# Windowed attention into an RWKV feed-forward block on one core: the squared keys of the beginning rounded on ScalarE, and the beginning's order written anew

## The chip, the cores and the metric

The kernel runs on one core of a Trainium2 chip. The metric is the device time of one execution in microseconds (us); lower is better. The engines are named as the profile names them: PE is TensorE, which multiplies matrices (PEld is its loading of weights); DVE is VectorE, ACT is ScalarE, POOL is GpSimd, and SP is the engine whose queue issues the transfers. All run side by side, each works through its own queue in order, and they wait for each other by semaphores.

## The reference

Eight batches, eight heads of width 64, 512 local tokens and 32 global ones. Local tokens attend to the global ones and to a window of 32 tokens on each side; global tokens attend to all. What comes out, transposed to tokens by 512 channels, goes through an RWKV channel mix whose value product has the squared keys as input. Cut to what matters:

```python
s_g = scale * q_g @ k_all.T;            out_g = softmax(s_g) @ v_all
s_l = concat(scale * q_l @ k_g.T, where(|i - j| <= 32, scale * q_l @ k_l.T, -1e9))
out_l = softmax(s_l) @ concat(v_g, v_l)
x = concat(out_g, out_l) as (8, 544, 512)       # x_prev: x one token earlier
xk = mu_k * x + (1 - mu_k) * x_prev;    xr = mu_r * x + (1 - mu_r) * x_prev
k = maximum(xk @ w_k, 0)                        # 512 -> 1024
out = sigmoid(xr @ w_r) * ((k * k) @ w_v)       # 512 -> 512, 1024 -> 512
```

## The kernel before

Operands of the feed-forward products are split in two: a high part, rounded to the format fp32r that PE reads, and a low part, the remainder. Each product is then three matmuls: high by high, high by low, low by high. So for a squared key `k2` there are `kkh` (`k2` rounded to fp32r) and `kkl` (`k2 - kkh`); for a mixed input `xkh`, `xkl`, `xrh`, `xrl`; for the weights `wk_h`, `wk_l` and so on. The weights come as 64-bit numbers in 20 chunks of 512 columns and are turned into such pairs on the chip.

The work has a beginning and a steady part. In the beginning, batch 0 is read, attended and mixed, its first keys and gates are computed, batch 1's attention is begun and the 20 chunks of weights are made ready, all interleaved. The steady part takes batches 1 to 7 in loops. The order of the beginning is a string of steps, run one after the other; each appends its instructions to the queues of its engines. So a step's place decides what stands ahead of it on every queue that it uses. A step is a name and its indices. The names that matter here:

- `S`, `G`: scores (PE), per unit of two heads and per half of its blocks, and global scores; `R`, `g`: their scaling and row minimum into `Pt` and `Pg` (DVE); `E`, `X`: exponentials (ACT); `I`, `i`: inverse sums (DVE); `N`, `n`: normalizing (POOL); `T`, `H`: transposes (PE); `C`, `h`: copies of these into `PT` (ACT); `W`: products with the values (PE); `O`: their copies into `xT` (ACT). Without a 1 they belong to batch 0; `S1`, `R1`, `E1`, `T1` and the like to batch 1.
- `c`: load of a weight chunk (SP); `a` and `e`: its two steps on ACT (`L240`, and `L254`, the cast to the high part); `b` and `d`: its two on DVE (`L244`, `L249`); `f`: its low part (POOL, `L258`). Chunks 0 to 7 are `w_k`, 8 to 11 `w_r`, 12 to 19 `w_v`.
- `kd`, `kx`, `kc`, `kl` (token half, first of two groups of channels): the token mix for the keys. `kd` is the difference (DVE, `L665`), `kx` the mix (DVE, `L672`), `kc` the cast to the high part (DVE, `L678`), `kl` the low part (POOL, `L682`). `rd`, `rx`, `rc`, `rl` are the same for the gates.
- `Ka`, `Kb` (half, f): the two halves of a key product (PE, twelve matmuls each); `kr`: relu (ACT, `L618`); `qm`: the square (POOL, `L623`); `z`: the two parts `kkh` and `kkl` (DVE, `L629`, `L630`).
- `Qa`, `Qb`, `y`: gate products (PE) and their tanh (ACT); `Va`, `Vb`, `vo`: value products and the write of a result. `L1`, `M1`: loads of batch 1's queries and keys, and values.

What a step waits for beside its data is a buffer. PSUM has eight banks; in the beginning the products "m" have two, "s" four, and "t" two (`T`, `H`, `W`, part of `G` and, for the second token half, `kd` and `rd` use "t"). The tiles `xfull`, `relu` and `k2` share three buffers, and the weight chunks from the fifth on share four.

Of the kernel before, what the change touches and what calls it, by code (L numbers as in the profile page):

```python
# [69 lines left out]
def local_global_attention_then_rwkv_ffn(  # L70
# [498 lines left out]
    class Tokens:  # L569


        def __init__(self, cur, prev, shape, store):
# [4 lines left out]
        def two(self, pool, name, dtype=F32, tag="tmp"):
# [40 lines left out]
            nc.scalar.activation(self.rk[f0], self.kp.pop(f0), AF.Relu)  # L618

        def key_square(self, f0):  # L620
            rk = self.rk.pop(f0)
            self.k2[f0] = self.two(tmpp, "k2")
            nc.gpsimd.tensor_mul(self.k2[f0], rk, rk)  # L623

        def key_parts(self, f0):
            kh = self.two(mlp, "kkh", F32R, f"kkh{f0}")
# [2 lines left out]
            nc.vector.tensor_copy(kh, k2)  # L629
            nc.vector.tensor_sub(kl, k2, kh.bitcast(F32))  # L630
# [490 lines left out]
    for step in """
        q.0 v.0 q.1 v.1 q.2 v.2 q.3 v.3 mu S.0,0,0 masks c.3 c.0 R.0,0,0 c.1 c.2 E.0,0,0 c.4 S.0,1,0 c.5 c.6 c.8
        R.0,1,0 S.0,0,1 E.0,1,0 G.0 R.0,0,1 E.0,0,1 S.0,1,1 g.0 L1.0 I.0,0 X.0 R.0,1,1 S.1,0,0 N.0,0,1 i.0
        S.1,1,0 E.0,1,1 n.0 N.0,0,0 H.0,0 H.0,1 h.0,0 I.0,1 N.0,1,0 h.0,1 T.0,0,0 T.0,0,1 C.0,0,0 N.0,1,1
        S.1,0,1 C.0,0,1 R.1,0,0 T.0,1,0 S.1,1,1 C.0,1,0 R.1,0,1 T.0,1,1 E.1,0,0 R.1,1,0 G.1 E.1,0,1 R.1,1,1 g.1
        a.3 b.3 X.1 I.1,0 d.3 N.1,0,1 a.0 i.1 b.0 e.3 N.1,0,0 C.0,1,1 d.0 a.1 b.1 W.0,0 f.3 e.0 d.1 E.1,1,0 f.0
        b.2 e.1 b.4 n.1 O.0,0 f.1 b.5 a.2 T.1,0,0 H.1,0 kd.0,0 a.4 C.1,0,0 d.2 h.1,0 T.1,0,1 kx.0,0 e.2 H.1,1
# [222 lines left out]
```

## Time and profile before

| | |
|---|---|
| device time, 3 runs | 645.59, 645.38, 642.23 us, median 645.38 |
| the profiled execution | 643.38 us, of which the span of its instructions 641.6 us |
| PE busy | 617.7 us, 96% of the span |
| DVE, ACT, POOL busy | 80%, 52%, 54% |
| granted clock of TensorE | 0.987 of full speed on the mean; below full in three stretches |
| transfers | 127.13 MB, 198 GB/s on the mean |

From about 92 us on, PE is busy without a break until near the end. Nearly all its idle time and the two long stretches at half clock lie in the beginning, which the change rearranges. The forty slices of the page show this: PE's row reads `5698899999999999999999999999999999999997`, sixteen us a slice. In a timeline, "idle before <- releaser" is what ended the wait.

### The profile page before, as it was taken

What the parts mean: (1) busy time and instruction counts of PE and PEld (TensorE: products, weight loads), DVE (VectorE), ACT (ScalarE), POOL (GpSimd) and SP (SyncE); (2) the same over time, 40 slices, a digit from 0 to 9 for tenths busy, and PEclk for the clock granted to TensorE, in tenths of its full rate; (3) what the DMA queues carried; (4) which work ended last, traced back from release to release, by engine and by line L of the source; (5) the groups of instructions that cost most, each with busy time, mean ns of one, the idle gap of its engine ahead of it and who ended that gap; (6) DMA issues with size and microseconds to landing.
All of it is one profiled execution on the core that took longest, in us unless ns stands there. A gap on an engine that the chain in (4) does not pass through costs nothing.

```text
span 641.6 us, 20381 instructions
## 1 busy us (share of the span) xinstructions
PE 617.7 (96%) x8304; PEld 591.6 (92%) x8304; DVE 515.4 (80%) x1312; ACT 333.9 (52%) x1054; POOL 348.5 (54%) x319
## 2 busy tenths in 40 slices
PE   5698899999999999999999999999999999999997
PEld 3577789999999999999999999999999999999997
DVE  3787999657897699987799697987799677787981
ACT  5996677446273667363746537372746433314211
POOL 6575767436856253765357534755367425652840
PEclk9787999999999999999999999999999999999999
DMA  8944545428356924737373675647372662462775
GB/s 363 368 172 194 179 145 178 155 68 321 122 199 213 340 120 166 231 122 264 143 277 133 238 270 197 214 167 269 121 287 80 214 214 68 148 206 107 234 232 191
DMA packets 43564, 127.13 MB, mean 198 GB/s; under 512 B 4048, under 2 KB 20944, under 8 KB 43472
## 3 DMA queue, kind: packets, MB, share of 16 engines
q1 hardware_dynamic: 43472, 125.85, 55.8%
q8 instruction: 65, 1.06, 0.7%
q14 instruction: 27, 0.22, 0.1%
HBM read 108.53 MB, written 17.30 MB: 196 GB/s over the span
## 4 chain that ended last, share of the span: by engine, by line
PE 88%; DVE 6%; ACT 3%; POOL 2%; issue 1%; POOLq 0%; DVEq 0%; ACTq 0%
PE ps_m L142 68%; PE ps_s L142 12%; PE ps_t L145 5%; PE ps_t L142 1%; DVE Pt L378 1%; ACT Pt L385 1%; DVE kkl L630 1%; DVE ps_t L665 1%; POOL masks L171 1%; DVE kkh L629 1%; DVE xfull L672 1%; POOL Pt L396 0%; ACT wk_h L254 0%; DVE Pg L448 0%; DVE ps_s L665 0%
## 5 line engine op out<-in xcount | busy, mean ns | idle before, releaser
L142 PE MATMUL ps_m<-xkh,wk_h 128*128 128x256 f32 x544 | 155.2, 285 | 0.0
L142 PE MATMUL ps_m<-xkl,wk_h 128*128 128x256 f32 x544 | 151.0, 278 | 0.0
L142 PE MATMUL ps_m<-xkh,wk_l 128*128 128x256 f32 x544 | 150.9, 277 | 0.0
L142 PE MATMUL ps_m<-bh,a 128*128 128x256 f32 x736 | 136.4, 282 | 0.1
L396 POOL TENSOR_TENSOR Pt<-Pt,ssum 128x512 f32<-128x512 f32 x64 | 70.5, 1106 | 94.1 <-DVE ssum L339 60.2
L142 PEld LDWEIGHTS ps_m<-bh,a 128*128 128x128 f32 x736 | 114.7, 189 | 0.3 <-DVE xrh L607 0.3
L385 ACT ACTIVATE Pt<-Pt,m 128x128 f32<-128x128 f32 x256 | 99.4, 392 | 20.2 <-DVE m L378 19.9
L142 PEld LDWEIGHTS ps_m<-xkh,wk_h 128*128 128x128 f32 x544 | 102.5, 188 | 4.0 <-issue 1.4
L142 PEld LDWEIGHTS ps_m<-xkh,wk_l 128*128 128x128 f32 x544 | 102.7, 189 | 0.0
L142 PEld LDWEIGHTS ps_m<-xkl,wk_h 128*128 128x128 f32 x544 | 102.7, 189 | 0.0
L142 PE MATMUL ps_m<-bl,a 128*128 128x256 f32 x368 | 102.6, 279 | 0.0
L142 PE MATMUL ps_m<-xrh,wr_h 128*128 128x256 f32 x272 | 77.0, 283 | 1.0 <-ACT relu L618 1.0
L142 PE MATMUL ps_m<-xrl,wr_h 128*128 128x256 f32 x272 | 75.5, 277 | 0.0
L142 PE MATMUL ps_m<-xrh,wr_l 128*128 128x256 f32 x272 | 75.4, 277 | 0.0
L608 POOL TENSOR_TENSOR xkl<-xfull,xkh 128x512 fp32r<-128x512 f32 x30 | 39.9, 1331 | 60.8 <-DVE xkh L607 33.3
L419 ACT COPY PT<-ps_t 128x512 f32<-128x512 f32 x56 | 32.7, 583 | 76.6 <-PE ps_t L145 76.4
L713 ACT ACTIVATE relu<-ps_m 128x512 f32<-128x512 f32 x52 | 30.7, 591 | 79.8 <-PE ps_m L142 77.6
L142 PEld LDWEIGHTS ps_m<-bl,a 128*128 128x128 f32 x368 | 69.2, 188 | 0.0
L378 DVE CUSTOM_DVE_ANT_0 Pt<-ps_s,masks 128x128 f32<-128x128 f32 x256 | 55.8, 285 | 11.2 <-PE ps_s L142 8.1
L608 POOL TENSOR_TENSOR xrl<-diff,xrh 128x512 fp32r<-128x512 f32 x30 | 41.0, 1368 | 37.9 <-DVE xrh L607 27.6
L798 POOL TENSOR_TENSOR bl<-B,bh 128x512 fp32r<-128x512 f32 x36 | 51.9, 1458 | 16.1 <-DVE bh L797 16.1
L142 PE MATMUL ps_s<-raw_qk 64*32 64x128 f32 (+1 forms) x2112 | 51.7, 287 | 7.6 <-DMA raw_qk<-qk 6.4
(127 smaller groups left out, 1508.2 us busy)
## 6 DMA issues: line engine op xcount, KB each, us to landing
a<-scratch SPq DMA_DIRECT2D x92, 512.0 KB, 4.7
raw_v<-v SPq DMA_DIRECT2D x32, 896.0 KB, 7.3
raw_qk<-qk SPq DMA_DIRECT2D x32, 624.0 KB, 5.4
out_l<-gate SPq DMA_DIRECT2D x32, 256.0 KB, 3.9
w<-w_k SPq DMA_DIRECT2D x8, 512.0 KB, 9.7
w<-w_v SPq DMA_DIRECT2D x8, 512.0 KB, 3.2
w<-w_r SPq DMA_DIRECT2D x4, 512.0 KB, 5.9
scratch<-wv_h SPq DMA_DIRECT2D x8, 256.0 KB, 3.9
```

The source lines that it names most:

```text
L142: return in_line(nc.tensor.matmul(*a, **kw))
L145: return in_line(nc.tensor.transpose(*a, **kw))
L171: nc.gpsimd.affine_select(out=m, in_=m, pattern=[[i - c, CK]], base=0, channel_multiplier=c - i, compare_op=ALU.is_ge, fill=NEG,)
L378: nc.vector.tensor_tensor_reduce(out=self.Pt[:, i], in0=self.place(t, n, h), in1=masks[self.slots[t][1]][:, n], op0=ALU.add, op1=ALU.min, ...
L385: nc.scalar.activation(self.Pt[:, i], self.Pt[:, i], AF.Exp, bias=self.low[:, i:i + 1], scale=-1.0, accum_out=self.sum[:, i:i + 1],)
L396: nc.gpsimd.tensor_mul(self.Pt[:, some], self.Pt[:, some], inv.unsqueeze(2).to_broadcast([P, 4, W]))
L419: nc.scalar.copy(pitched(j, h, 0, 4), tp.rearrange("p (g q) -> p g q", g=4))
L608: nc.gpsimd.tensor_sub(lo[:, both], xf, hi[:, both].bitcast(F32))
L629: nc.vector.tensor_copy(kh, k2)
L630: nc.vector.tensor_sub(kl, k2, kh.bitcast(F32))
L713: nc.scalar.activation(rk, kp, AF.Relu)
L798: (nc.vector if b[0] == "B" else nc.gpsimd).tensor_sub(l, val, h.bitcast(F32))
```

## The change

The rounding of the eight squares `k2` of batch 0 to `kkh` leaves DVE. ACT squares the relu a second time (`key_high`, step `zh`) and writes the result straight in fp32r, so that the write rounds it. `k2` is still made by POOL, and DVE's step `z` keeps only the subtraction `k2 - kkh`. The relu tile therefore stays in use until both POOL and ACT have read it. Besides, the string that orders the beginning is another one throughout; it has the same steps and eight more, the `zh`. The steady part is untouched.

```diff
         def key_square(self, f0):
-            rk = self.rk.pop(f0)
+            rk = self.rk[f0]
             self.k2[f0] = self.two(tmpp, "k2")
             nc.gpsimd.tensor_mul(self.k2[f0], rk, rk)
+        def key_high(self, f0):
+            self.kh[f0] = self.two(mlp, "kkh", F32R, f"kkh{f0}")
+            nc.scalar.activation(self.kh[f0], self.rk[f0], AF.Square)
+
         def key_parts(self, f0):
-            kh = self.two(mlp, "kkh", F32R, f"kkh{f0}")
+            kh = self.kh.pop(f0)
             kl = self.two(mlp if f0 + 2 < NF else mlp1, "kkl", F32R, f"kkl{f0}")
             k2 = self.k2.pop(f0)
-            nc.vector.tensor_copy(kh, k2)
             nc.vector.tensor_sub(kl, k2, kh.bitcast(F32))
...
+        "zh": lambda t, f: first[t].key_high(f),
...
-        d.4 C.1,0,1 f.2 h.1,1 kc.0,0 e.4 W.1,0 a.5 f.4 b.6 a.6 d.5 E.1,1,1 d.6 kl.0,0 c.7 S1.0,0 b.8 O.1,0
-        rd.0,0 Ka.0,0 I.1,1 e.5 rx.0,0 N.1,1,1 e.6 W.0,1 R1.0,0 a.8 f.5 a.7 Ka.0,2 N.1,1,0 rc.0,0 c.9 E1.0,0,0
-        M1.0 f.6 S1.0,1 d.8 O.0,1 I1.0,0,0 kd.0,2 early_w e.8 rl.0,0 T.1,1,0 c.10 G1.0 E1.0,0,1 kx.0,2 kc.0,2
-        L1.1 f.8 a.9 I1.0,0,1 g1.0 C.1,1,0 T.1,1,1 X1.0 kl.0,2 c.11 R1.0,1 C.1,1,1 N1.0,0,1 W.1,1 i1.0 E1.0,1,0
...
+        f.2 c.9 O.1,0 I.1,1 b.7 a.7 Ka.0,2 kd.0,2 e.6 N.1,1,1 a.8 W.0,1 d.7 kx.0,2 e.7 N.1,1,0 a.9 rx.0,0 f.6
+        O.0,1 M1.0 kc.0,2 T.1,1,0 f.7 c.10 T.1,1,1 C.1,1,0 rc.0,0 C.1,1,1 kl.0,2 W.1,1 d.8 early_w e.8 rd.0,2
+        rl.0,0 Kb.0,0 O.1,1 rx.0,2 G1.0 rc.0,2 f.8 kr.0,0 Kb.0,2 zh.0,0 g1.0 qm.0,0 c.11 Ka.0,4 c.12 rl.0,2
+        z.0,0 a.10 S1.0,0 kr.0,2 Kb.0,4 b.9 X1.0 qm.0,2 b.10 zh.0,2 Ka.0,6 d.9 a.11 z.0,2 kr.0,4 e.9 d.10 qm.0,4
+        Kb.0,6 zh.0,4 R1.0,0 e.10 f.9 a.12 kr.0,6 z.0,4 f.10 S1.0,1 c.13 E1.0,0,0 b.11 Qa.0,0 kd.1,0 L1.1
+        E1.0,0,1 qm.0,6 c.14 Qa.0,2 d.11 zh.0,6 kx.1,0 e.11 z.0,6 a.13 f.11 R1.0,1 Qb.0,0 c.15 I1.0,0,1 E1.0,1,0
...
```

Three places show how this moves instructions. The first is ACT ahead of the product `W.1,1`, batch 0's last value product. Before, `L454` (the exponential of batch 1's global scores, `X1.0`) stands between the two copies `L423` (`C.1,1,0` and `C.1,1,1`) that `W.1,1` needs:

```order
L254 CAST wr_h<-w_321 128x512
L385 ACTIVATE Pt,ssum<-Pt,m 128x128 x4
L240 ACTIVATE w_867<-w_867 128x512
L423 COPY PT<-ps_t 128x2x2x128
L454 ACTIVATE Pg,ssumg<-Pg,mg 128x544
L423 COPY PT<-ps_t 128x2x2x128
```

In the change the two copies stand together, right behind the six copies of `O.0,1`, with `e.7` (`w_683`) and `a.9` (`w_758`) ahead of these:

```order
L254 CAST wk_h<-w_683 128x512
L240 ACTIVATE w_758<-w_758 128x512
L539 COPY xT<-ps_t 128x2x64
L542 COPY xT<-ps_t 128x2x32
L549 COPY xT<-ps_t 128x64
L539 COPY xT<-ps_t 128x2x64
L542 COPY xT<-ps_t 128x2x32
L549 COPY xT<-ps_t 128x64
L423 COPY PT<-ps_t 128x2x2x128 x2
L254 CAST wr_h<-w_319 128x512
```

So the exponential left the gap between the copies, and a chunk's step came ahead of the copies before them.

The second is DVE at the same time, at the mix of the first token half's upper channels (`kd.0,2`, `L665`; in the change these lines have numbers three higher). Before, it stands behind the reads of batch 1's first scores (sixteen rows `L378`, not shown) and these:

```order
L678 CAST xrh<-xfull 128x512
L249 SCALAR_TENSOR_TENSOR w_321<-w_321,ps_s 128x512
L338 TENSOR_SCALAR ssum<-ssum 128x4
L339 RECIPROCAL ssum<-ssum 128x4
L665 TENSOR_TENSOR ps_s<-xT 128x256 x2
L672 SCALAR_TENSOR_TENSOR xfull<-ps_s,mu_k_sb,xT 128x256 x2
L678 CAST xkh<-xfull 128x512
```

In the change it follows the inverse sums of batch 0's last scores (`I.1,1`) and `b.7`; `d.7` (`w_683`), which ACT's `e.7` needs, comes behind it:

```order
L338 TENSOR_SCALAR ssum<-ssum 128x8
L339 RECIPROCAL ssum<-ssum 128x8
L244 TENSOR_SCALAR ps_s<-w_683 128x512
L668 TENSOR_TENSOR ps_s<-xT 128x256 x2
L249 SCALAR_TENSOR_TENSOR w_683<-w_683,ps_s 128x512
L675 SCALAR_TENSOR_TENSOR xfull<-ps_s,mu_k_sb,xT 128x256 x2
L675 SCALAR_TENSOR_TENSOR xfull<-ps_s,mu_r_sb,xT 128x256 x2
L681 CAST xkh<-xfull 128x512
```

The eight score reads and one pair of inverse sums went from ahead of it to behind it.

The third is ACT some 15 us later, at the relus of the first keys. Before, the cast `e.11` of the last gate weights (`w_974`) comes right behind the second relu (`L618`):

```order
L254 CAST wr_h<-w_867 128x512
L618 ACTIVATE relu<-ps_m 128x512
L254 CAST wr_h<-w_974 128x512
L240 ACTIVATE w_1144<-w_1144 128x512
L618 ACTIVATE relu<-ps_m 128x512
L482 COPY PT<-ps_t 96x4x2x32
L488 COPY PT<-ps_t 64x4x32
L385 ACTIVATE Pt,ssum<-Pt,m 128x128 x4
```

In the change the same cast (`w_957` there) comes behind the fourth relu, eight exponentials and the fourth new square (`L627`):

```order
L618 ACTIVATE relu<-ps_m 128x512
L254 CAST wr_h<-w_758 128x512
L627 ACTIVATE kkh<-relu 128x512
L254 CAST wr_h<-w_852 128x512
L240 ACTIVATE w_972<-w_972 128x512
L618 ACTIVATE relu<-ps_m 128x512
L385 ACTIVATE Pt,ssum<-Pt,m 128x128 x8
L627 ACTIVATE kkh<-relu 128x512
L254 CAST wr_h<-w_957 128x512
```

So the gate weights' last cast moved behind two more relus, three squares and eight exponentials.

More of the change, by code (lines that the diff above doesn't have):

```diff
@@ L573, in __init__ @@
             self.cur, self.prev, self.shape, self.store = cur, prev, shape, store
-            self.kp, self.rk, self.k2, self.rp, self.vp, self.x, self.d = ({} for _ in range(7))
+            self.kp, self.rk, self.k2, self.rp, self.vp, self.x, self.d, self.kh = ({} for _ in range(8))
             self.kk_h, self.kk_l = [], []
@@ L1121, in local_global_attention_then_rwkv_ffn @@
     for step in """
[L1122 to L1123 removed]
+        q.0 v.0 q.1 q.2 v.1 v.2 q.3 v.3 mu S.0,0,0 masks c.3 c.0 R.0,0,0 c.1 c.4 E.0,0,0 c.5 S.0,1,0 c.6 c.8 c.2
+        R.0,1,0 S.0,0,1 E.0,1,0 G.0 R.0,0,1 E.0,0,1 S.1,0,0 g.0 S.0,1,1 I.0,0 L1.0 X.0 R.0,1,1 N.0,0,1 i.0
         S.1,1,0 E.0,1,1 n.0 N.0,0,0 H.0,0 H.0,1 h.0,0 I.0,1 N.0,1,0 h.0,1 T.0,0,0 T.0,0,1 C.0,0,0 N.0,1,1
@@ L1145, in local_global_attention_then_rwkv_ffn @@
-        f.18 W1.1 N1.2,0,0 e.19 I1.2,1,1 E1.2,1,0 f.19 E1.2,0,1 N1.2,1,1 I1.2,1,0 Vb.0 N1.2,1,0 M1.2 O1.1
-        I1.2,0,1 N1.2,0,1 Vb.2 vo.0 z.1,6 vo.2
+        a.3 b.3 X.1 I.1,0 d.3 N.1,0,1 a.0 b.0 e.3 N.1,0,0 i.1 d.0 C.0,1,1 a.1 b.1 W.0,0 f.3 e.0 d.1 E.1,1,0 b.4
+        n.1 f.0 e.1 b.5 O.0,0 f.1 b.6 a.5 T.1,0,0 H.1,0 kd.0,0 a.4 C.1,0,0 d.4 h.1,0 H.1,1 kx.0,0 e.4 T.1,0,1
+        d.5 a.2 f.4 b.2 h.1,1 C.1,0,1 kc.0,0 e.5 c.7 W.1,0 d.2 kl.0,0 a.6 b.8 e.2 d.6 E.1,1,1 f.5 rd.0,0 Ka.0,0
+        f.2 c.9 O.1,0 I.1,1 b.7 a.7 Ka.0,2 kd.0,2 e.6 N.1,1,1 a.8 W.0,1 d.7 kx.0,2 e.7 N.1,1,0 a.9 rx.0,0 f.6
@@ new lines, in local_global_attention_then_rwkv_ffn @@
+        i1.0 kd.1,2 N1.0,0,1 b.12 S1.1,0 kx.1,2 E1.0,1,1 n1.0 Qb.0,2 I1.0,1,0 kc.1,2 N1.0,1,0 kc.1,0 a.14 G1.1
+        y.0,0 kl.1,2 a.15 I1.0,1,1 T1.0,1,0 I1.0,0,0 g1.1 C1.0,1,0 kl.1,0 y.0,2 H1.0,0 rd.1,0 N1.0,1,1 Ka.1,0
+        X1.1 rx.1,0 h1.0,0 i1.1 N1.0,0,0 Ka.1,2 rc.1,0 rd.1,2 T1.0,1,1 rl.1,0 Kb.1,0 C1.0,1,1 rx.1,2 rc.1,2
+        T1.0,0,0 kr.1,0 H1.0,1 Kb.1,2 rl.1,2 C1.0,0,0 h1.0,1 d.12 zh.1,0 qm.1,0 T1.0,0,1 kr.1,2 b.14 Ka.1,4
+        C1.0,0,1 R1.1,0 zh.1,2 Qa.1,0 early_u e.12 f.12 z.1,0 E1.1,0,1 Kb.1,4 c.16 E1.1,0,0 d.14 Qb.1,0 qm.1,2
@@ new lines, in local_global_attention_then_rwkv_ffn @@
+        b.13 I1.1,0,1 kr.1,4 d.13 S1.1,1 N1.1,0,1 y.1,0 z.1,2 zh.1,4 Qa.1,2 L1.2 e.13 I1.1,0,0 qm.1,4 b.16 a.16
+        Ka.1,6 b.15 e.14 f.13 d.16 Qb.1,2 d.15 e.16 f.14 c.18 R1.1,1 e.15 Kb.1,6 y.1,2 f.16 c.17 W1.0 N1.1,0,0
+        kr.1,6 E1.1,1,0 f.15 z.1,4 zh.1,6 c.19 a.18 b.18 qm.1,6 E1.1,1,1 T1.1,0,0 M1.1 I1.1,1,0 Va.0 d.18
+        N1.1,1,0 e.18 I1.1,1,1 O1.0 N1.1,1,1 n1.1 T1.1,1,0 Va.2 a.19 b.17 f.18 C1.1,1,0 b.19 a.17 d.19 C1.1,0,0
+        d.17 e.19 T1.1,0,1 e.17 f.19 T1.1,1,1 S1.2,0 C1.1,0,1 C1.1,1,1 f.17 H1.1,0 R1.2,0 S1.2,1 h1.1,0 H1.1,1
@@ L1147, in local_global_attention_then_rwkv_ffn @@
+        Vb.0 h1.1,1 R1.2,1 E1.2,0,0 E1.2,0,1 I1.2,0,0 W1.1 N1.2,0,0 vo.0 E1.2,1,0 E1.2,1,1 I1.2,1,0 N1.2,1,0
+        Vb.2 M1.2 O1.1 I1.2,1,1 N1.2,1,1 G1.2 z.1,6 vo.2 g1.2 X1.2 I1.2,0,1 N1.2,0,1 i1.2 n1.2
     """.split():
```

15 lines of the change are left out of this document (removed).

## The prediction

> **What bounds the kernel now.** I read the stretches first, then PE's timeline, then the chain of waits, then the queues of the engines that PE waits for. The stretches are cut at four events of the beginning: the end of `W.0,1`, the first `Kb`, the first `Ka` of the second token half, the first value product. Columns: stretch, length, then busy us (instructions) of PE, PEld, DVE, ACT, POOL, then granted clock, DMA share and GB/s.
>
> ```profile
> 24.00:42.00 18.00, 14.43 (x282) 12.98 (x282) 15.72 (x46) 17.61 (x64) 13.32 (x12) 0.72 0.53 208
> 42.00:54.10 12.10, 8.55 (x149) 6.75 (x148) 11.23 (x38) 7.87 (x34) 8.57 (x8) 0.79 0.97 380
> 54.10:79.20 25.10, 23.07 (x288) 20.06 (x288) 21.57 (x50) 16.81 (x51) 14.91 (x12) 0.96 0.41 141
> 79.20:105.80 26.60, 25.33 (x405) 24.10 (x403) 26.11 (x75) 19.55 (x51) 19.57 (x17) 1.00 0.39 131
> 105.80:121.00 15.20, 15.20 (x215) 14.94 (x210) 9.28 (x36) 11.54 (x50) 9.35 (x9) 1.00 0.69 249
> ```
>
> PE is the bound from 105.8 on. Before that DVE is nearly full (26.11 of 26.60 us in the fourth row) while PE has gaps of 3.55, 2.03 and 1.27 us in rows two to four, and the clock is below full in rows one to three. All that this change can win in the stretches it mainly alters is there: 6.85 us of gaps and what the clock costs. PE's rows name the waits:
>
> ```profile
> 34.36 3.10 PE L142 MATMUL ps_t<-PT,raw_v 128*64 128x96 f32 x80 [0.18 <-ACT PT L423]
> 40.04 2.05 PE L142 MATMUL ps_t<-PT,raw_v 128*64 128x32 f32 x56
> 45.45 0.98 PE L142 MATMUL ps_s<-raw_qk 128*64 128x480 f32 x4
> 48.72 0.30 PE L142 MATMUL ps_t<-PT,raw_v 128*64 128x32 f32 x2 [1.27 <-DVE mg L448]
> 50.93 3.25 PE L142 MATMUL ps_t<-PT,raw_v 128*64 128x32 f32 x54 [1.91 <-ACT PT L423]
> 71.67 0.38 PE L142 MATMUL ps_m<-xrh,wr_h 128*128 128x256 f32 x1 [0.96 <-ACT relu L618]
> 88.67 0.66 PE L145 MATMUL ps_t<-ident,Pt 128*128 128x128 f32 x4 [1.27 <-POOL Pt L396]
> ```
>
> The row at 45.45 is most of `G1.0`. Those at 48.72 and 50.93 are `W.1,1`: 3.18 us of waiting, for a PSUM bank and for a copy. The chain of waits (start, us) shows which engine sets the pace after that, and the price of blocks of matmuls:
>
> ```profile
> 54.18 2.42 PE ps_m L142 x12
> 58.50 1.54 DVE kkh L629
> 65.73 1.49 DVE kkh L629
> 70.25 0.86 DVE kkh L629
> 74.74 0.34 DVE kkh L629
> ...
> 80.69 0.20 DVE Pt L378
> ...
> 101.42 1.38 PE ps_m L142 x12
> 103.13 1.09 PE ps_s L142 x64
> 121.44 0.44 PE ps_t L145 x4
> ```
>
> Four casts to `kkh`, 4.23 us, lie on the chain. Twelve matmuls cost 2.42 us in the stretch with the reduced clock and 1.38 later; `W.1,1` took 3.25 us and the same product `W.0,1` 2.05. So half speed cost 1.04 + 1.20 = 2.24 us here.
>
> **The casts.** Eight go from DVE, eight squares come to ACT; the first two rows group DVE's cast and subtraction, the third is the same square in the steady part, the last two are what POOL did under the first pair:
>
> ```profile
> L629 DVE CAST kkh<-k x8: 410/1098/1529, 58.5 to 119.3; 128x512 fp32r<-128x512 f32 x8
> L630 DVE TENSOR_TENSOR kkl<-k,kkh x8: 691/1568/1776, 60.1 to 121.4; 128x512 fp32r<-128x512 f32 x8
> L715 ACT ACTIVATE B<-relu x52: 630/632/638, 211.8 to 617.3; 128x512 f32<-128x512 f32 x52
> 58.42 1.32 POOL L258 TENSOR_TENSOR wk_l<-w,wk_h 128x512 fp32r<-128x512 f32 x1
> 59.69 1.47 POOL L682 TENSOR_TENSOR xrl<-xfull,xrh 128x512 fp32r<-128x512 f32 x1
> ```
>
> A cast takes 0.41 us alone and up to 1.53 when a POOL instruction runs: the one at 58.50 ended 0.3 us after POOL's of 58.42 did. DVE is freed of 8 x 0.41 to 8 x 1.53, 3.3 to 12.2 us, near 8 by the median of 1.10. ACT gets 8 x 0.63 = 5.1 us, in a queue that was busy 16.81 of 25.10 and 19.55 of 26.60 us, so it has room on the mean. On the path this is worth no more than PE's gaps after 54 us, 2.03 + 1.27: PE had other work under the rest of those 4.23 us.
>
> The Trainium skill speaks against even that (page SBUF — State Buffer, section Who interferes with whom): a DVE cast, and a DVE operation with two SBUF inputs, share a port with GpSimd, and the later one waits for the earlier whole instruction. By that rule the remaining subtraction waits where the cast waited, and only 8 x 0.41 us are surely won. The rows agree that both stretch, 0.41 to 1.53 and 0.69 to 1.78. My sum does not rest on it, since I follow the queues below.
>
> **The order, to `Kb.0,0`.** In the change PE does `Ka.0,0`, `Ka.0,2`, `W.0,1`, `T.1,1,0`, `T.1,1,1`, `W.1,1`, `Kb.0,0`; the two score products `S1.0` and `G1.0` come later. From the end of `W.1,0` (34.36 + 3.10, taken as 37.4) PE has 2 x 1.38 + 2.05 us and is free at 42.2. `T.1,1,0` needs a bank that `O.0,1` empties, and `O.0,1` stands on ACT behind `e.7` and `a.9`. Rows for this walk:
>
> ```profile
> 38.76 0.20 DVE L339 RECIPROCAL ssum<-ssum 128x8 f32<-128x8 f32 x1
> 44.07 2.81 DVE L665 TENSOR_TENSOR ps_s<-xT 128x256 f32<-128x256 f32 x2
> L244 DVE TENSOR_SCALAR ps_s<-w x16: 676/684/712, 28.3 to 109.6; 128x512 int32<-128x512 int32 x16
> L254 ACT CAST wk_h<-w x8: 652/662/710, 24.8 to 57.2; 128x512 fp32r<-128x512 f32 x8
> L240 ACT ACTIVATE w<-w x20: 652/686/784, 22.7 to 109.7; 128x512 f32<-128x512 f32 x20
> 42.64 0.29 ACT L539 COPY xT<-ps_t 128x128 f32<-128x128 f32 x1
> 43.25 0.28 ACT L549 COPY xT<-ps_t 128x64 f32<-128x64 f32 x1
> 50.31 0.56 ACT L423 COPY PT<-ps_t 128x512 f32<-128x512 f32 x1
> 37.71 0.94 DVE L665 TENSOR_TENSOR ps_s<-xT 128x256 f32<-128x256 f32 x2
> ```
>
> `I.1,1` ends at 38.96 as before, then DVE has `b.7` 0.68, `kd.0,2` 0.94 to 2.81 (I take 1.5, nearer the undisturbed pair since fewer POOL instructions lie under it), `d.7` 0.68, to 41.8; ACT has `e.7` 0.66, `a.9` 0.69, the six copies 42.64 to 43.53 = 0.89, to 44.05; then a transpose 0.44 and two copies 1.12: `W.1,1` starts at 45.6, with PE idle 45.6 - 42.2 - 0.88 = 2.5 us against 3.55 before. Gain 1.05, with the ends of `kd.0,2` 1.6 to -0.25. On the clock: it fell after the waits of 1.27 and 1.91 us, so it will probably fall after 2.5, but once, since no second wait follows. I take a loss of 1.5 for the 2.24 of before; ends 0 and 2.24. **Gain to here 1.8, between -0.25 and 3.8.** What covers the moved `S1.0` and `G1.0` is that they fill PE later, one for one.
>
> The Trainium skill (TensorE: Matmul & The Clock Gate, section HAM oscillation) says that the clock falls when PE idles for more than about 3.4 us. By that the gap of 2.5 would cost nothing, and the sum would be 1.5 us better. The trace does not agree: the block of 2.42 us ran at half speed though no wait before it reached 3.4 us (1.27 and 1.91).
>
> **From `Kb.0,0` to `Ka.1,0`.** Before, this took the 25.1 us of the third stretch, for some 20.2 us of matmuls: ten blocks of 1.38, five groups of transposes of 0.44 at most, two score products of 1.09, two global ones of 0.98. Lost are 4.9, of which 1.04 is the clock counted above; 3.85 are left. In the change two waits stand out. `Qb.0,0` needs `f.11` on POOL, behind `e.11`, behind the square `zh.0,6`, behind eight exponentials, behind `kr.0,6`, which waits for `Kb.0,6`:
>
> ```profile
> L385 ACT ACTIVATE Pt<-Pt,m 128x128 f32<-128x128 f32 x256 | 99.4, 392 | 20.2 <-DVE m L378 19.9
> L258 POOL TENSOR_TENSOR wr_l<-w,wr_h x4: 1296/1404/1768, 45.1 to 75.0; 128x512 fp32r<-128x512 f32 x4
> ```
>
> With a relu at the square's 0.63, that is 0.63 + 8 x 0.39 + 0.63 + 0.66 + 1.40 = 6.4 us after `Kb.0,6`, less some 0.3 where ACT's instructions overlap; PE has `S1.0,1` 1.09 and two blocks of 1.38 to do, 3.85, and part of `Qb`: a wait of 2.0. `Ka.1,0` needs `kl.1,0`. After `zh.0,6` (4.2) DVE has a subtraction 0.69, eight reads of 0.21, three inverse sums 1.0, a difference 1.5, `b.12` 0.68, a mix no longer than the pair's undisturbed 0.94 and two casts 0.82; then POOL has two low parts of 1.3: 14 us after `Kb.0,6`. PE arrives 2.8 earlier, part of it already waiting for a transpose. Together 4.8 us, with PE's own small gaps inside them. **A loss of 4.8 - 3.85, about 1.0; the ends are a gain of 3.85, if PE never waits, and a loss of 2.3, if the difference takes 2.81.** The relief of DVE does not show here because `z.0,6` now waits for ACT.
>
> **From `Ka.1,0` to the value products.** The 1.27 us before 88.67 was a transpose that waited for POOL; in the change it comes behind the first value product. I found no new wait: `W1.0` needs the banks of `S1.1,1`, which DVE has read by then. **Gain 1.27; at the other end a new wait as long as the old two of 1.27 and 1.91 less it, a loss of 1.9.**
>
> **Sum.** 1.8 - 1.0 + 1.27 = 2.1 us, from the profiled execution's 643.38: 641.3. Its median of three is 645.38, 2.0 above it, the lowest 642.23. About 0.5%, 3.2 us, is what a measurement of this kernel can tell from no change.
>
> **Rivals.** *No gain:* `kd.0,2` takes 2.81 again, `W.1,1` waits as long and the clock falls for as long; then -0.25 - 1.0 + 1.27, with what DVE saves hidden under PE's other work: about 643.4. For it: the waits moved, their lengths are alike. *All waits go:* DVE, freed of some 8 us, reaches `kc.1,0` early, and PE hardly waits after 42 us: 3.8 + 1.9 (half of the second term's best) + 1.27 = 7.0, 636.4. For it: DVE lay on the chain; against it: ACT's exponentials stand ahead of `zh.0,6`. *The clock stays full* after the gap of 2.5 us, and the rest is as in the sum: 1.5 more, 639.8; for it, the gap stands alone, where before two came together; against it, the fall before. (It is what the page on the clock gate would have.) *Slower:* the transfers of `w_v`. On SP `L1.2` now stands ahead of `c.18`, `c.17`, `c.19`, and its second load waits for `S1.1,1`; `c.19` also for the buffer of `f.15`.
>
> ```profile
> w<-w_v SPq DMA_DIRECT2D x1, 512.0 KB, 3.1
> ```
>
> From the end of `f.15` it takes 3.1 + 0.69 + 0.66 + 0.66 + 2 x 1.3 = 7.7 us till the last low part, and `Vb.0` follows `Va.0` by four blocks of 1.38, two score products and five groups of transposes, some 10 us. So it costs from the point where `f.15` ends more than about 2.3 us after `Va.0` could start, then us for us; with an overrun of 6 and the sum above, 647.
>
> **Chances.** The sum's course 0.38; no gain 0.25; all waits go 0.15; the clock stays full 0.09; slower 0.13. Faster by over 0.5% are the case without waits, the one with the full clock, and 0.16 of the sum's course, which by its own ends can gain over 3.2: 0.40. Slower 0.13, the rest 0.47 the same. The range goes from 636.5, where nearly all waits are gone, to 646.0, no gain and the median's offset; the likeliest case alone 639 to 643.5.
>
> **What would show it.** In the profile after: no `L629` on DVE, eight squares of 0.63 us on ACT; `W.1,1` at 44.5 to 47 with one wait before it; a half-clock stretch shorter than before; PE waiting for POOL's `wr_l` ahead of `Qb.0,0` and for `xkl` ahead of `Ka.1,0`, 4 to 5 us together; no wait of 1 us after that. Wrong would be: no waits in the middle, or one ahead of `Vb.0`.

## The result, and the profile after

The changed kernel takes 648.3 us in the median of 18 runs, the kernel before 644.07 in the median of 18 beside it; the ratio is 1.005, with a 95% interval of 1.0035 to 1.0064. It is slower, by some 3 us, where 2 us of gain were forecast. A second set of 12 runs gave 646.04 us and a ratio of 1.0028 [1.0005 to 1.0052]. Each ratio is to runs of the kernel before beside that set. The profiled execution of the change took 645.9 us (span 644.1), that of before 643.38 (641.6).

The same five stretches of time as in the prediction, after the change; the events that cut them lie elsewhere now (length, then busy us of PE, PEld, DVE, ACT, POOL, granted clock, DMA share, GB/s):

```profile
24.00:42.00 18.00, 13.76 (x160) 12.38 (x161) 16.82 (x30) 16.22 (x59) 13.82 (x12) 0.57 0.61 239
42.00:54.10 12.10, 10.80 (x161) 9.26 (x160) 9.85 (x17) 7.20 (x22) 7.93 (x7) 0.93 0.74 277
54.10:79.20 25.10, 20.15 (x322) 17.58 (x321) 24.42 (x71) 19.18 (x57) 17.36 (x15) 0.97 0.43 144
79.20:105.80 26.60, 26.58 (x358) 25.84 (x357) 21.86 (x67) 20.81 (x65) 18.52 (x16) 0.96 0.46 142
105.80:121.00 15.20, 15.20 (x320) 14.22 (x319) 6.91 (x42) 13.17 (x54) 7.08 (x7) 1.00 0.35 122
```

Over the five DVE is busy 4.1 us less than before: the eight casts, 7.8 us, are gone, but the sixteen subtractions of the mix (`kd`, `rd`) take 3.6 us more. In the fourth row DVE is relieved, 21.86 us instead of 26.11, and PE has next to no gap left. But in the third PE is busy 20.15 us where it was 23.07, with DVE nearly full (24.42 of 25.10), and the clock of the first fell from 0.72 to 0.57. PE's rows that answer to those shown of before:

```profile
34.63 5.17 PE L142 MATMUL ps_t<-PT,raw_v 128*64 128x96 f32 x80 [0.67 <-ACT PT L482]
44.49 1.85 PE L142 MATMUL ps_t<-PT,raw_v 128*64 128x32 f32 x56
47.22 1.06 PE L145 MATMUL ps_t<-ident,Pt 128*128 128x128 f32 x8 [0.88 <-ACT xT L549]
48.52 0.30 PE L142 MATMUL ps_t<-PT,raw_v 128*64 128x32 f32 x2 [0.24 <-ACT PT L423]
49.01 1.85 PE L142 MATMUL ps_t<-PT,raw_v 128*64 128x32 f32 x54 [0.19 <-ACT PT L423]
50.78 0.38 PE L142 MATMUL ps_m<-xkh,wk_h 128*128 128x256 f32 x1
66.78 0.39 PE L142 MATMUL ps_m<-xrh,wr_h 128*128 128x256 f32 x1 [0.61 <-ACT wr_h L254]
68.62 0.39 PE L142 MATMUL ps_m<-xrh,wr_l 128*128 128x256 f32 x1 [1.34 <-POOL wr_l L258]
74.08 0.65 PE L145 MATMUL ps_t<-ident,Pt 128*128 128x128 f32 x4 [0.66 <-POOL Pt L396]
77.07 0.53 PE L145 MATMUL ps_t<-ident,Pg 128*96 128x128 f32 x3 [2.33 <-DVE mg L448]
```

The row at 34.63 is `W.1,0`: 5.17 us instead of 3.10. At 48.52 and 49.01 stands `W.1,1`, with almost no wait before it now, and at full clock (1.85 us, before 3.25). `Kb.0,0` starts at 50.78, before at 54.11, but 3.3 us of score products that were done by then before come later now. Then four waits that were not there, 4.94 us together.

To add up such things I use one figure throughout, the *loss* of a stretch: PE's idle time plus half of its busy time at half speed, from the 12th us on. PE has the same matmuls to do in both orders, so this is, near enough, the time that the order costs.

| loss, us | 12 us to `Kb.0,0` | to `Ka.1,0` | to the first value product | to 130 us | sum |
|---|---|---|---|---|---|
| before | 16.4 | 2.9 | 1.3 | 0 | 20.6 |
| the change | 16.3 | 4.95 | 1.7 | 0.4 | 23.4 |

The difference of 2.8 us is close to the 2.5 us by which the profiled executions differ, and it has all arisen by the first square: that of the steady part (line `L715`, in the change `L718`) starts at 211.8 us before and 214.4 after, and from there on both run alike, to the last one at 617.3 and 619.8.

```profile
L718 ACT ACTIVATE B<-relu x52: 630/632/637, 214.4 to 619.8; 128x512 f32<-128x512 f32 x52
```

The chain of waits shows who sets PE's pace between 62 and 77 us, after the change (start, us):

```profile
63.40 0.87 DVE ps_t L668
64.30 1.15 DVE ps_t L668
...
70.01 1.15 DVE ps_t L668
...
72.81 1.50 DVE xkh L681 x2
74.31 1.16 DVE ssum L338
75.67 1.02 DVE ssum L338
77.07 0.53 PE ps_t L145 x3
```

No cast to `kkh` is on it any more. In their place are differences of the mix (`L668`) and two additions on 128x4 numbers (`L338`) that take as little as 0.14 us elsewhere and took 1.2 and 1.1 here, with POOL busy beside them. DVE itself waits for nothing that counts between 54.3 and 90.0 us: these are all its waits of 0.15 us or more from 54.3 to 91 us.

```profile
61.00 1.79 DVE L633 TENSOR_TENSOR kkl<-k,kkh 128x512 fp32r<-128x512 f32 x1 [0.19 <-POOL k L623]
90.02 0.83 DVE L338 TENSOR_SCALAR ssum<-ssum 128x4 f32<-128x4 f32 x1 [1.21 <-ACT Pt L385]
```

The granted clock by stretches, after (the window's length, PE's busy time, ..., clock):

```profile
26.60:36.80 10.20, 8.01 (x91) 6.69 (x89) 9.52 (x16) 10.00 (x33) 7.22 (x7) 0.50 0.61 242
36.90:40.20 3.30, 3.30 (x53) 3.24 (x52) 3.23 (x6) 1.77 (x13) 2.53 (x3) 0.50 0.54 187
40.30:43.60 3.30, 3.30 (x18) 3.30 (x17) 2.94 (x6) 2.90 (x10) 3.28 (x3) 0.50 0.06 22
74.40:77.70 3.30, 0.97 (x10) 0.73 (x8) 3.09 (x7) 2.14 (x3) 3.30 (x4) 1.00 0.58 192
77.80:81.10 3.30, 3.30 (x18) 3.30 (x17) 3.20 (x10) 1.36 (x4) 0.90 (x2) 0.50 0.00 0
```

Half speed lasts from 26.6 to 43.6 us (before 25.2 to 35.4), the stretch at 49 to 56 is gone, and a new one of 3.4 us follows the waits ahead of `Ka.1,0`.

### The profile page after: what moved, and what is told of

Read it like the earlier page. It is cut to its first block, busy times and chain, and to the rows that moved or that the text cites. A ratio compares the mean times of both kernels' runs of the same rounds, so it can differ in the third digit from the quotient of the medians.

```text
span 644.1 us, 20392 instructions
## 1 busy us (share of the span) xinstructions
PE 620.3 (96%) x8304; PEld 594.2 (92%) x8304; DVE 513.3 (80%) x1304; ACT 338.3 (53%) x1062; POOL 349.9 (54%) x319
## 3 DMA queue, kind: packets, MB, share of 16 engines
q8 instruction: 65, 1.06, 0.7%
## 4 chain that ended last, share of the span: by engine, by line
PE 91%; DVE 3%; ACT 2%; POOL 2%; issue 1%; POOLq 0%; ACTq 0%; DVEq 0%
PE ps_m L142 70%; PE ps_s L142 13%; PE ps_t L145 6%; PE ps_t L142 2%; DVE Pt L378 1%; POOL masks L171 1%; ACT Pt L385 1%; DVE ps_t L668 1%; DVE ssum L338 0%; ACT wk_h L254 0%; ACT PT L423 0%; POOL Pt L396 0%; DVE xkh L681 0%; DVE xfull L675 0%; DVE kkl L633 0%
## 5 line engine op out<-in xcount | busy, mean ns | idle before, releaser
L142 PEld LDWEIGHTS ps_m<-xkh,wk_h 128*128 128x128 f32 x544 | 103.8, 191 | 3.6 <-issue 1.9
L378 DVE CUSTOM_DVE_ANT_0 Pt<-ps_s,masks 128x128 f32<-128x128 f32 x256 | 55.7, 286 | 14.3 <-PE ps_s L142 11.2
L608 POOL TENSOR_TENSOR xrl<-diff,xrh 128x512 fp32r<-128x512 f32 x30 | 41.1, 1370 | 37.3 <-DVE xrh L607 27.3
```

Source lines behind the costliest of these rows:

```text
L142: return in_line(nc.tensor.matmul(*a, **kw))
L378: nc.vector.tensor_tensor_reduce(out=self.Pt[:, i], in0=self.place(t, n, h), in1=masks[self.slots[t][1]][:, n], op0=ALU.add, op1=ALU.min, ...
L608: nc.gpsimd.tensor_sub(lo[:, both], xf, hi[:, both].bitcast(F32))
```

## The experiments

**The square apart from the order.** `e1` has the order of before with the squares on ScalarE; `e2` the new order with the casts on VectorE; `e3` and `e4` cross the two orders at `W.1,0`.

```diff
e1  steps of before; behind each qm.t,f:  + zh.t,f
e2  steps of the change without zh;  z: + nc.vector.tensor_copy(kh, k2)
e3  steps up to W.1,0 as in before, the others in the order of the change
e4  steps up to W.1,0 as in the change, the others in the order of before, with zh
```

> The order of before, with the squares on ScalarE alone (each placed right behind POOL's square of the same tile). Theory A, the loss of 4.2 us (644.1 to 648.3) is PE's clock under the new order, a first half-speed stretch that lasts 17.1 us instead of 10.2 and a new one of 3.4 at Ka.1,0: this kernel has neither, its half-speed stretches stay at 25-35 and 49-56, and it takes 641 to 644.5, since up to 2 us of the casts' 4.2 on the chain come off. Theory B, the squares themselves cost it, by 8 x 0.63 us in ScalarE's queue ahead of what PE waits for: 647 to 648.5. Theory C, the loss is the waits of the new order behind Kb.0,0 alone (1.9 at Qb.0,0, 3.0 ahead of Ka.1,0): as A, 641 to 644.5.

> The order of after, with the casts on VectorE as before and no squares on ScalarE. A: the beginning up to Kb.0,0 has no cast in it, so the clock loss of some 4 us stays, and the four casts of the first half delay VectorE further; 648 to 651. B: without the squares the loss goes, 643.5 to 645.5. C: the waits behind Kb.0,0 grow by 1 to 4 us, since VectorE is the one that reads g1.1 and makes xkh late: 649 to 652, but with a beginning no slower than in before.

> Steps up to W.1,0 in the order of before, all others in the order of after. A: if the order of the first 37 us sets how long the clock stays at half, it ends at about 35 as in before, W.1,0 takes 3.1 us instead of 5.2, the two Ka's 1.4 each, and the kernel takes 644 to 645.5. If it stays down to 42-44 here too, then what comes behind W.1,0 decides it or it is chance from execution to execution, and the time is 647 to 648.5. C: the waits behind Kb.0,0 are untouched, 647.5 to 648.5. B: 648.

> The counterpart: steps up to W.1,0 in the order of after, all others in the order of before, with the squares on ScalarE. A: half speed to about 43, the other waits as in before: 646 to 648. C: no loss without the new order behind Kb.0,0: 642 to 644.5. B: 647 to 648.5.

| | median, us | ratio to before, 95% interval | first steady square, us |
|---|---|---|---|
| e1, square alone | 642.18 | 0.9971 [0.995, 0.9992] | 210.2 |
| e2, order alone | 650.08 | 1.0096 [1.0059, 1.0132] | 217.2 |
| e3, old start, new rest | 649.17 | 1.0078 [1.0049, 1.0107] | 217.1 |
| e4, new start, old rest | 645.73 | 1.001 [0.999, 1.003] | 210.5 |

The square is not the loss: alone it gains 0.3%, some 2 us. Of PE's waits after 54 us the 1.27 is gone, those of 0.96 and 1.01 are 0.42 and 0.51, and one of 0.41 came. The order is the loss, 6 us without the square. In the traces the greater part hangs on what comes behind `W.1,0`: the first steady square is 6.9 us later in e3 than in e1, and 3.9 later in the change than in e4. The start alone is not settled: e4 against e1 is 2 to 3 us in the ratios, but 0.3 in the two traces. Theory B is out, and A, that the order of the first 37 us sets the clock, is not saved: e3 has the old start and the full clock again by 35 us, and is no faster. It is no test of a full clock, since it fell to half speed again from 45.2 to 55.5 and from 72.5 to 75.9 us. Theory C, the waits behind `Kb.0,0`, comes nearest: e2 has the four of the change, grown to 6.3 us, and e4 has none of them; but e3 and e4 both came out above the times that C gave.

**The clock.** `e6` takes away the pause of 0.67 us ahead of `W.1,0`; `e7` fills PE's pauses of 3.5 and 1.4 us with transposes that nothing uses; `e8` does the same in e1's order; `e0` is the change once more.

```diff
e6  - ... d.5 a.2 f.4 b.2 h.1,1 C.1,0,1 ...
    + ... d.5 f.4 b.2 h.1,1 C.1,0,1 a.2 ...
e7  groups(0, shared)                       # W.0,0 only
    + keep_warm(28, both[0])
    groups(0, alone); groups(1, alone); groups(1, shared)
    + keep_warm(18, rest_bank)
```

> The change, with a.2 on ScalarE moved behind the two copies h.1,1 and C.1,0,1, so that W.1,0 comes straight behind the transposes instead of 0.67 us later. Theory A1, the clock's first half-speed stretch is longer in the new beginning since this pause breaks the one dense stretch (30.4 to 34) that could lift it before W.1,0: half speed ends some 7 us earlier in most runs, the granted clock goes from 0.984 to 0.986 to 0.989, and the time falls by 2 to 3.5 us, to 644.5 to 646.5. Rival, the pause has nothing to do with it (where the 3.41-us grid happens to lie, or other work): clock 0.984 and 647.5 to 648.5, 0.6 us better at most.

> The change, with 28 transposes of the identity into an unused quarter of a PSUM bank between the first 24 and the other 56 matmuls of W.0,0, and 18 more behind W.0,0, where TensorE is idle for 3.5 and 1.4 us. They add nothing to the result. Theory A: with no pause over 0.5 us the clock stays full from 13 to 47; W.1,0 takes 2.05 to 3.1 us instead of 5.2, Ka.0,0 and Ka.0,2 take 2.8 instead of 4.7; granted clock 0.992 to 0.995; 3 to 4 us at Kb.0,0 are won if TensorE sets the pace there, 644 to 645.5. Rival, the other engines set the pace to W.1,1 (kd.0,2 and e.8, O.0,1 on their queues): the clock is full, but TensorE waits as much longer ahead of T.1,1,0, and the time is 647 to 648.5. If the filler does not hold the clock, the half-speed stretch stays, and the time is 648 to 649.

> The order of before with the squares on ScalarE (as in the kernel that took 642.2) and the same 28 + 18 transposes of the identity. A: its first half-speed stretch (27.3 to 34.1 in the profile, a loss of 2.2 us by the ledger of pauses and half-speed time) goes, 640 to 641.5; the second one at 51 to 58 stays. Rival, other engines set the pace to W.1,1: 642 to 643.

> The change itself once more, as the measure for the two beside it: 646 to 649. In its profile the half-speed stretch of the beginning may lie elsewhere. If the loss to 50 us (pauses plus half the time at half speed, 13.0 in the first profile) hangs on the clock's chance, it comes out 2 us or more away from 13; if it hangs on the order, it stays within 0.5.

e6: 649.15 us, 1.0064 [1.0042, 1.0087]. e7: 649.6 us, 1.0082 [1.0061, 1.0104], with a granted clock of 0.986 to 0.992 in its runs. e8: 644.27 us, 0.9989 [0.997, 1.0007], no gain on e1 though its clock is 0.994 on the mean of its runs. The profile of e6 says why. Its clock was full from 34.5 to 44.7; `W.0,1` ran at 40.47 instead of 44.49, and then PE stood still:

```profile
40.47 1.85 PE L142 MATMUL ps_t<-PT,raw_v 128*64 128x32 f32 x56
45.54 1.94 PE L145 MATMUL ps_t<-ident,Pt 128*128 128x128 f32 x8 [3.22 <-POOL wk_l L258]
```

`T.1,1,0` needs the bank that the copies `O.0,1` empty, and it starts 0.10 us after the last of them in both profiles (the POOL instruction named in the row is not what it needs). What ACT waited for ahead of these copies differs. In the change it was PE, late by its clock; in e6 it was DVE's `d.7`, which the cast `e.7` ahead of the copies reads. First the change, then e6:

```profile
46.01 0.27 ACT L539 COPY xT<-ps_t 128x128 f32<-128x128 f32 x1 [1.59 <-PE ps_t L142]
```

```profile
43.44 0.66 ACT L254 CAST wk_h<-w 128x512 fp32r<-128x512 f32 x1 [1.90 <-DVE w L249]
```

Of 4 us won 1.7 were left at `T.1,1,0`, and with this pause the clock fell again (1.94 us for eight transposes instead of 1.06), from 44.7 to 54.9, so that `Kb.0,0` came at 51.34 and `Ka.1,0` at 79.52, 0.6 and 2.2 us later than in the change. In e7 and e0 (in this order) the same transposes came about where they came in the change, at 47.22, though `W.1,0` had begun 2 us later; ACT waited for `d.7` there too:

```profile
36.80 4.66 PE L142 MATMUL ps_t<-PT,raw_v 128*64 128x96 f32 x80 [1.15 <-ACT PT L482]
47.42 1.06 PE L145 MATMUL ps_t<-ident,Pt 128*128 128x128 f32 x8 [1.16 <-POOL wk_l L258]
```

```profile
36.63 4.91 PE L142 MATMUL ps_t<-PT,raw_v 128*64 128x96 f32 x80 [0.66 <-ACT PT L482]
47.28 1.06 PE L145 MATMUL ps_t<-ident,Pt 128*128 128x128 f32 x8 [1.04 <-POOL wk_l L258]
```

In e0 the half-speed stretches lay elsewhere (17.2 to 20.6, 27.4 to 41.1, 68.4 to 71.8), and its loss from 12 us to `Kb.0,0` is 16.4, in the first profile 16.3, in e2, e5 and e6 16.3 to 16.4. So theory A falls for this part: up to `Kb.0,0` the order sets the loss, and whether it shows as half speed or as waiting differs from execution to execution. e7 and e8 are no clean tests of the full clock, since filler and a half-speed stretch at 17 to 21 and 16 to 19 us made the work before `W.1,0` late.

**The wait ahead of `Ka.1,0`.**

```diff
- ... zh.0,6 kx.1,0 e.11 z.0,6 a.13 f.11 R1.0,1 ... kc.1,2 N1.0,1,0 kc.1,0 a.14 G1.1 y.0,0 ... g1.1 C1.0,1,0 kl.1,0 ... Ka.1,0
+ ... zh.0,6 kx.1,0 kc.1,0 e.11 z.0,6 a.13 f.11 kl.1,0 R1.0,1 ... kc.1,2 N1.0,1,0 a.14 y.0,0 G1.1 Ka.1,0 g1.1 ...
```

> The change, with four steps of the middle moved: kc.1,0 right behind kx.1,0 on VectorE, kl.1,0 right behind f.11 on GpSimd, Ka.1,0 and g1.1 right behind G1.1 (TensorE and VectorE). Theory A2, the waits of 0.66 and 2.33 us ahead of Ka.1,0 and the half-speed stretch that follows them are a loss of the new order: the first half of the keys starts near 73.5 instead of 77.4, no stretch at half speed follows, and the kernel takes 3 to 4.5 us less than the change, 643.5 to 645.5. Rival, another wait is hidden right behind (the bank that y.0,0 empties on ScalarE, or kl.1,2 for Kb.1,0): the same work starts no more than 1 us earlier, 647 to 648.5.

646.14 us, 1.0028 [1.0015, 1.0042]; beside the change's 1.005 and 1.0028 no gain is shown. `Ka.1,0` did start at 73.52 instead of 77.36 and no half speed followed. Then the next transposes and the next key product waited 0.84 and 0.85 us, for POOL's `Pt` and for ACT's gate, and the two transposes behind them waited for DVE:

```profile
80.23 0.63 PE L145 MATMUL ps_t<-ident,Pt 128*128 128x128 f32 x4 [0.76 <-DVE ssumg L338]
83.58 0.63 PE L145 MATMUL ps_t<-ident,Pt 128*128 128x128 f32 x4 [1.34 <-DVE xfull L675]
```

They need the PSUM banks in which DVE keeps the differences `rd.1,0` and `rd.1,2`, and each comes 0.14 us after the mix that frees its bank (`L675`, which end at 80.09 and 83.44). In the change these transposes stand at 81.80 and 83.80. By the loss: 1.9 instead of 4.95 up to `Ka.1,0`, and 3.8 instead of 1.7 from there to the value products, which start at 102.53 instead of 102.76: 0.2 us are left. Theory A2 falls. The rival, another wait hidden right behind, is right in kind but not in size (it had the keys start no more than 1 us earlier, and 647 to 648.5): the wait taken away came back at the next steps.

The last of these waits is in e0 too, which is the change itself:

```profile
83.86 0.63 PE L145 MATMUL ps_t<-ident,Pt 128*128 128x128 f32 x4 [1.33 <-DVE xfull L675]
```

e0 has no half speed after `Ka.1,0`, and PE waits; the change has, and PE does not wait; both reach this transpose at the same time, 83.86 and 83.80 us. So do they reach the transposes behind `g1.1`, at 77.13 and 77.07, though only e0 ran at half speed from 68.4 to 71.8. With DVE at work from 54.3 to 90.0 in both, with no wait but the 0.19 us, DVE paces this stretch, and the clock of PE at 78 us cost nothing there.

**The moved scores.** `e9` puts the next unit's first scores back; `e10` takes one other part of the new order, `G1.0` late, into e1.

```diff
e9  + S1.0,0 behind kl.0,0;  R1.0,0 behind I.1,1;  E1.0,0,0 behind O.0,1;  E1.0,0,1 behind e.8   (and removed where they stood)
e10 + G1.0 behind W.1,1;  g1.0 behind rd.0,2;  X1.0 behind a.10;  i1.0, n1.0 behind rx.0,2       (in the order of before)
```

> The change, with the first scores of the next unit put back where before had them, ahead of Ka.0,0: S1.0,0 on TensorE (64 matmuls, 1.1 us), R1.0,0 on VectorE (eight reads, 1.7 us) behind I.1,1, the eight exponentials E1.0,0,0 and E1.0,0,1 (3.1 us) on ScalarE behind O.0,1 and e.8. Theory D, the loss comes from this move: up to W.1,1 TensorE waits for the other engines anyhow, so the products stood there for nothing, and behind Kb.0,0 they and the chain that hangs on them (reads, exponentials ahead of zh.0,6 and e.11) are paid in full. Then the pause ahead of Qb.0,0 (0.6 + 1.3 us) goes or shrinks to 0.5, and the kernel takes 2 to 4 us less than the change: 644.5 to 646.5. Rival E, the other steps behind W.1,0 are to blame (kd.0,2 and the weights' steps ahead of Ka.0,2): the pause goes, but the exponentials delay O.1,1 and kr.0,0 by their 3.1 us, and it is 647.5 to 650.

> The order of before with the squares on ScalarE (642.2 us), and of the new order one part alone: G1.0 with g1.0, X1.0, i1.0 and n1.0 behind W.1,1 and Kb.0,0 instead of ahead of them. It takes away the pause for the bank that G1.0 holds (0.88 us in the profile) and lets T.1,1,1 and W.1,1 follow at once; G1.0's 1.0 us is then paid behind Kb.0,0. Theory D (a product that fills a wait is free, and paid when it is moved behind it): no gain, 641.5 to 643.5. Rival, W.1,1's pauses are worth what they last: Kb.0,0 starts 2 to 3 us earlier, the half-speed stretch at 51 to 58 is shorter, 639 to 641.

e9: 648.41 us, 1.0075 [1.0045, 1.0105]. Theory D falls here: the waits at `Qb.0,0` are still 0.56 and 1.35 us. The rival E has the time (647.5 to 650), but it had the waits go as well. The transposes `T.1,1` come 1.5 us later, of which 0.8 were there at `W.1,0`, ahead of all that was moved. e10: 642.08 us, 0.997 [0.9952, 0.9987], the same as e1, as theory D had it for this step. `W.1,1` began at 47.24 instead of 48.51, and a wait of 1.47 us came ahead of `G1.0` instead (at 51.70).

**The differences of the mix under GpSimd.** In the new order the sixteen subtractions `kd`, `rd` take 15.5 us of DVE (8.4 + 7.1), with e1's order 11.1 (6.5 + 4.6). `e11` (order of the change), `e12` (order of before, squares on ScalarE) and `e13` (e12 with e10) write them so that no step reads two large tiles of SBUF, the memory that is not PSUM (a step that makes `rest` is left out):

```diff
-  nc.vector.tensor_sub(d, cur, prev);            xf = d * mu + prev
+  nc.vector.tensor_scalar(d, cur, mu, None, op0=ALU.mult);   xf = prev * rest + d      # rest = 1 - mu, 32 bytes
```

> The change, with the sixteen subtractions of the mixing (rows L668 of the change, two SBUF inputs each, 15.5 us between 24 and 125 in two profiles of it, 11.1 with the order of before) written another way: mu times the token from one SBUF input, and (1 - mu) times the token before it added in the next step, which reads one SBUF and one PSUM input. Theory F, the order of the change loses time because it puts these subtractions under GpSimd's instructions, where a pair takes up to 2.65 us instead of 0.94, and VectorE sets the pace to the value products: they shrink to 8 x 0.9 = 7 us, kd.0,2, d.7 and O.0,1 come 2 us earlier, and the kernel takes 3 to 5 us less than the change (646 to 648.3), 642 to 644.5. Rival, the loss is the order itself on whatever engine (ScalarE's exponentials ahead of zh.0,6 and e.11, g1.1 late): 1.5 us less at most, 645 to 647.

> The same rewriting of the subtractions in the order of before with the squares on ScalarE (642.2 us). Theory F: there they cost 11.1 us, of which 4 go, and little of it is on the way: 640.5 to 642, so that the distance to the same rewriting in the order of the change (before: 3.9 us at the first square of the steady part) shrinks to 2 or less. Rival: both kernels gain alike, and the distance stays near 4.

> The kernel with the order of before, squares on ScalarE and rewritten subtractions, and G1.0 with its steps behind Kb.0,0 besides. VectorE reaches d.7 and ScalarE O.0,1 earlier, so that W.1,1, no longer behind G1.0's bank, starts near 46: 638.5 to 641. If G1.0's place is worth nothing, as in the order without the rewriting: the same as its neighbour, 640.5 to 642.

653.9 us, 1.0133 [1.0098, 1.0168]; 648.96 us, 1.0058 [1.0038, 1.0078]; 651.25 us, 1.0089 [1.006, 1.0117]: all slower, for a reason that has nothing to do with the question. The steady part of e12 (first to last of the 52 squares) takes 412.4 us (e11 411.8, e13 410.9) instead of 405 to 408:

```profile
L722 ACT ACTIVATE B<-relu x52: 630/632/637, 207.7 to 620.1; 128x512 f32<-128x512 f32 x52
```

The new tile has 32 bytes, and in these three an unused tile further on (`shift_left`) was cut from 64 bytes to 32; by the order in which the kernel allots them, what lies between the two moved by 32 bytes (the traces hold no addresses). `e13` is not faster than e12 either, and its first steady square comes 4.2 us later. `e14` and `e15` are e12 and e11 again, with these 32 bytes inside the unused tile, which keeps its 64:

```diff
+  rest = pad[:, 0:2 * NC]      # pad: the 64 bytes "shift_left", there before and unused
```

> As the kernel with the order of before, squares on ScalarE and rewritten subtractions (648.96 us), but with the 32 bytes for 1 - mu inside a tile of 64 that was there unused, so that every other tile keeps its address. In the profile of its sister the steady part started 3.5 us earlier than with the squares alone, and then lost 8 us evenly to its end, with 116 to 118 ns from one matmul of 256 columns to the next where the others had 113 to 114. If that comes from the 32 bytes by which all tiles behind moved: a steady part as long as in the others, and 638 to 640. If the rewriting itself slows the steady part (more on VectorE, or other instructions): 648 to 650 again.

> The same rewriting at unmoved addresses in the order of the change. Theory F, the collision of the two-input subtractions with GpSimd is what the new order costs: 642 to 644.5, and within 2 us of its neighbour. If it is the order of the queues, as the beginning of its sister says (0.5 to 0.8 us earlier than the change at 121 to 153): 645.5 to 648, some 7 us behind its neighbour.

```profile
L723 ACT ACTIVATE B<-relu x52: 630/632/635, 207.2 to 614.4; 128x512 f32<-128x512 f32 x52
```

e14: 641.54 us, 0.9955 [0.9933, 0.9977]: the steady part is back at 407.2 us, so the place of these 32 bytes was it. This is the lowest median of the study, ahead of before by 3 us and of the change by more, though its interval overlaps those of e1 and e10. It missed its 638 to 640. e15: 646.14 us, 1.0032 [1.0014, 1.005]. The products take 0.46 to 0.49 us each whatever POOL does (the subtractions in the change 0.42 to 1.40), here in e15:

```profile
L671 DVE TENSOR_SCALAR ps_s<-xT,mu_k_sb x4: 486/487/487, 30.5 to 41.5; 128x256 f32<-128x256 f32 x4
L671 DVE TENSOR_SCALAR ps_s<-xT,mu_r_sb x4: 476/483/488, 37.5 to 46.7; 128x256 f32<-128x256 f32 x4
```

e14 and e15 still differ by 0.8%, as e1 and the change do by 0.6 to 0.8%: theory F falls as the cause of the new order's loss. What the collision costs either order is not settled. In the traces the first steady square comes 3.0 us earlier in e14 than in e1 and 4.1 earlier in e15 than in the change, but e15's profiled execution is the fastest of its twelve (642.82 us), and by the ratios neither gain is over 0.2%. That `T.1,1,0` came at 45.63 in e15, 1.6 us earlier than in the change, does not show it: half speed ended at 39.5 there, and in e11, with the same subtractions and half speed to 43.4, it came at 47.43.

## Why the prediction was wrong

**The squares: right in kind, small.** Eight squares on ScalarE, 0.62 to 0.65 us, none left on DVE; e1's gain of 0.3% lies within the bound of 2.03 + 1.27 us that was set for it. In the new order they are worth more (1.0096 without, 1.005 or 1.0028 with them, 3 to 4 us, though the intervals touch), because there DVE paces the middle.

**How the terms are counted.** The table above puts the 0.9 us that the reduced clock cost behind `Kb.0,0` into its second column; the prediction had them in its first term. Counted as the prediction does, the terms are a gain of 1.0 for 1.8, a loss of 2.9 for 1.0, and a loss of 0.9 for a gain of 1.27. The second and the third are the larger misses.

**First term, gain 1.8: measured 1.0** (0.1 in the table). The waits at `W.1,1` fell further than forecast, to 0.88 + 0.24 + 0.19 us for 3.55, where 2.5 were forecast, and the half-speed loss there went to nothing. But the walk began with "the end of `W.1,0`" ... "taken as 37.4" and "`I.1,1` ends at 38.96 as before", and neither held. `W.1,0` ended at 39.8, at half speed, and the two `Ka` took 4.7 us for the 2.76 assumed. On DVE `rd.0,0`, which now runs under two low parts of POOL, took 2.65 us instead of the 0.94 of the old row, so that `I.1,1` ended at 39.8 and `d.7` at 43.1 for the 41.8 forecast. In the change's trace the first of the two came last, since ACT waited 1.59 us for PE. Either alone was enough: with the clock full and DVE as late, the transposes came at 45.5 (e6). With the products in place of the subtractions, and half speed to 39.5 and 43.4 us, they came at 45.6 (e15) and 47.4 (e11), with ACT waiting for PE again. The forecast had 44.05, and `W.1,1` behind them. The step that failed is to take the part ahead of `W.1,1` as unchanged, although the order ahead of it was another too. One reading was off besides: the clock before fell at 49.1 us, after the wait of 1.27 us and as that of 1.91 began, so not after both.

**Second term, loss 1.0: measured 2.9** (2.0 in the table). Both waits came, in the forecast sizes: 0.61 + 1.34 us for 2.0 at `Qb.0,0`, through `zh.0,6`, `e.11` and `f.11`; and 0.66 + 2.33 for 2.8 ahead of `Ka.1,0`, though there by `g1.1` on DVE, which keeps the bank that `H1.0,0` needs, and not by `kl.1,0` (done 0.4 us earlier). What was mis-sized is the other side of the sum: 3.85 us "lost before" were taken from block prices and held PE's small gaps, which stay in the new order too. PE's idle time there was 2.03 us before and is 4.95 now.

**Third term, gain 1.27: measured a loss of 0.9.** The wait went. The step that failed is "I found no new wait": there is one, for DVE, which holds the banks that the next transposes need. In the change this does not show as a wait, because after the pause at 74 to 77 the clock fell for 3.4 us, 1.7 us of loss, which the forecast did not provide for either; e0 shows it as the wait of 1.33 us, at the same place and time. Another 0.4 us of waiting came at the end of the beginning, at 123.8 us.

**The signs and the rivals.** Of the signs named, the squares, the two waits of 4 to 5 us together (4.94) and no wait of 1 us after them came; `W.1,1` at 44.5 to 47 (48.5) and less time at half speed (20.5 us instead of 17.1) did not. Slower by `w_v`'s transfers did not happen; there is no wait ahead of `Vb.0`. "No gain", with the waits moved and as long, is nearest to what came. The Trainium skill (TensorE: Matmul & The Clock Gate, section HAM oscillation) has the clock fall when PE idles for more than about 3.4 us. Here it fell at 77.8 after waits of 0.66 and 2.33 us with matmuls between them, so the trace does not agree.

**Open.** That the loss comes from the order and not from the squares is shown (e1, e2), and that DVE paces PE from the middle to 84 us in the new order is shown by e0 beside the change. Which of DVE's steps make the loss is not: in the traces the order behind `W.1,0` costs some 4 us (e4 against the change), and no single step of it was found that gives them back (e5, e9, e15).
